# Softmaxed k times v: head pairs on the full array, or single heads on half of its columns

## The chip, the cores and the metric

The kernel runs on one core of one Trainium2 chip. The metric is device microseconds of one execution; before the change three runs gave 1338.9, 1341.31 and 1343.43 us, median 1341.31 us.

## The reference, cut to what matters

Attention with two softmaxes and no score matrix, then two MLPs over all 4608 tokens. Eight batches, eight heads each, 576 positions, 64 columns per head:

```python
q_s = softmax(q, axis=-1)           # over the 64 columns of a head
k_s = softmax(k, axis=2)            # over the 576 positions
kv  = np.einsum('bhsd,bhse->bhde', k_s, v)      # 64 x 64 for each batch and head
x   = np.einsum('bhsd,bhde->bhse', q_s, kv)     # then tokens x 512
h   = x @ w_in;   x = (relu(h) + alpha * min(h, 0)) @ w_out      # 512 -> 2048 -> 512
h   = x @ w_in2;  out = layer_norm(h * softmax(h)) * g @ w_out2  # 512 -> 1024 -> 512
```

## The kernel before

The instructions are written into a tile framework whose scheduler sets the order on each engine; each engine then works strictly in that order. Code order, buffer counts and the scheduler's own idea of what an operation lasts decide it.

The attention of batch 0 runs first, by itself (lines 781 to 833). The attention of batches 1 to 7 is cut into steps (`attention`, line 686) that line 718 (`slot`) strews between the matmuls of the first MLP's first phase: `g1` (lines 330 to 367) makes the hidden layer, `g2` (lines 421 to 432) adds it into the accumulators `acc`. Those matmuls carry single precision as two reduced parts, high and low, in three products.

For each batch and each group of four heads: `k_max` and `k_col` (lines 537 to 553) find the column maxima of k, with two transposes `mt` on TensorE; `k_exp` (line 555) spreads them with two transposes `mb` and writes e = exp(k - max). `k_v` (line 570) is what the change touches. The 576 positions lie as five slices r of 128 partitions, the last half filled with zeros in v. For two head pairs j and five slices r it multiplies the slice of e for two heads (128 columns, the stationary operand) with the slice of v for the same two heads (2 x 65 columns, the moving operand; the 65th column is ones and gives the softmax sum). The result of a pair is 128 x 130 in PSUM, tile `kv`: head one with its own v is the upper left quarter, head two with its own v the lower right one, and the other two quarters mix two heads and are not read. That is 10 matmuls in a `k_v`, and 16 `k_v` in the kernel. VectorE then adds 1e-9 to the sums (line 588), inverts them (589) and writes the two quarters, normalised, into `kvF` (592); `put` (line 123) splits that into the high and low halves `kk`, on ScalarE (124) and VectorE (125). `q_x` (line 657) multiplies `kk` with the transposed q (`qT`, from the transposes `qtp` of line 648) into `xp`, in the three matmuls of lines 662 to 664, the last of which needs the low half.

Batch 0's q softmax, second half, runs on ScalarE as 24 small activations (line 612).

Of the kernel before, what the change touches and what calls it, by code (L numbers as in the profile page):

```python
# [19 lines left out]
def attention_then_two_mlps(  # L20
# [32 lines left out]
    V, S, G, T = nc.vector, nc.scalar, nc.gpsimd, nc.tensor  # L53

    B, H, SQ, D = q.shape
# [21 lines left out]
    KB = SQ // P + 1  # L77
# [45 lines left out]
    def put(hi, lo, src, eng=V):  # L123
        S.activation(hi, src, AF.Copy)  # L124
        eng.tensor_tensor(lo, src, f32(hi), ALU.subtract)  # L125
# [375 lines left out]
    kts, vts = [kt, kt], [vt, vt]  # L501
# [68 lines left out]
    def k_v(b, g):  # L570
        et = A.pop(("e", b, g))
        js = slice(2 * g, 2 * g + 2)
        if g == 0:
            A["kk", b] = at.tile([P, 2, NP, P], F32R, tag="kk", name=f"kk_{b}")
        kk = A["kk", b]
        rk = at.tile([P, 2], F32, tag="rk", bufs=2, name=f"rk_{b}_{g}")
        t = ps_at.tile([P, 2, 2, D1], F32, tag="at", name=f"kv_{b}_{g}")
        for j in range(2):
            for r in range(KB):
                T.matmul(  # L580
                    t[:, j].rearrange("p a e -> p (a e)"),
                    et[:, r, 2 * j:2 * j + 2, :].rearrange("p h d -> p (h d)"),
                    vts[g][:, 2 * j:2 * j + 2, r, :],
                    start=r == 0, stop=r == KB - 1,
                )
        for a in range(2):
            pp_ = slice(a * D, (a + 1) * D)
            V.tensor_scalar_add(rk[pp_, :], t[pp_, :, a, D], 1e-9)
        V.reciprocal(rk, rk)
        for a in range(2):  # L590
            pp_ = slice(a * D, (a + 1) * D)
            V.tensor_tensor(
                kvF[pp_, js, a * D:(a + 1) * D], t[pp_, :, a, 0:D],
                rk[pp_, :].unsqueeze(2).to_broadcast([D, 2, D]), ALU.mult,
            )
        put(kk[:, 0, js], kk[:, 1, js], kvF[:, js])
# [89 lines left out]
    def attention(b):  # L686

        return [
            [lambda: k_max(b, 0)],
            [lambda: k_col(b, 0), lambda: q_max(b, 0)],  # L690
            [lambda: k_exp(b, 0), lambda: load_k(b, 1), lambda: q_exp(b, 0), lambda: load_q(b, 1)],
            [lambda: k_v(b, 0), lambda: load_v(b, 1), lambda: q_sum(b, 0)],
            [lambda: q_norm(b, 0), lambda: k_max(b, 1)],
            [lambda: k_col(b, 1), lambda: q_tr(b, 0, (0, 1)), lambda: q_max(b, 1)],
            [lambda: k_exp(b, 1), lambda: load_k(b + 1, 0), lambda: q_x(b, 0, (0, 1)),
             lambda: q_tr(b, 0, (2, 3)), lambda: q_exp(b, 1), lambda: load_q(b + 1, 0)],
            [lambda: k_v(b, 1), lambda: load_v(b + 1, 0), lambda: q_sum(b, 1)],
            [lambda: q_x(b, 0, (2, 3)), lambda: q_norm(b, 1)],
            [lambda: q_tr(b, 1, (0, 1))],
            [lambda: q_x(b, 1, (0, 1)), lambda: q_tr(b, 1, (2, 3))],  # L700
            [lambda: q_x(b, 1, (2, 3))],
        ]
# [108 lines left out]
    for g in range(2):  # L811
        k_v(0, g)
# [553 lines left out]
```

## Time and profile before

| what | value |
|---|---|
| median of three runs | 1341.31 us |
| the profiled execution, its span (the page gives no other time of its own) | 1341.7 us |
| TensorE busy | 1293.7 us, 96% |
| VectorE, ScalarE busy | 77%, 65% |
| mean granted TensorE clock | 0.987 |

TensorE's busy time counts each matmul from its start to a modelled end, and matmuls overlap: how fast they really follow each other is the distance between starts. A merged row of x20 matmuls lasts from the first start to the last end, so the distance between starts is its length less one matmul's length, over 19. A float32 matmul that is no transpose shows as two rows of the trace, two passes, each with its own weight load; a transpose and the matmuls of the MLPs show as one.

### The profile page before, as it was taken

The numbers are of one execution on the slowest core, as the hardware profiler recorded it, in microseconds if no ns is written. First come the engines' busy times: TensorE is split into PE (matmuls) and PEld (weight loads), VectorE is DVE, ScalarE is ACT, GpSimd is POOL, SyncE is SP. The second block draws the span as 40 slices with busy tenths as digits, with TensorE's granted clock in tenths as the row PEclk, the third lists the DMA queues.
The fourth block names the chain that finished last, engine by engine and source line by source line (L and its number), as shares of the span: only waits on it lengthen the run. The fifth ranks groups of instructions, "written<-read, shape, count | busy, mean of one in ns | idle before, by whom it ended". The sixth has DMA issues, their size and how long they took to land.

```text
span 1341.7 us, 21750 instructions
## 1 busy us (share of the span) xinstructions
PE 1293.7 (96%) x8188; PEld 1150.0 (86%) x8188; DVE 1036.5 (77%) x1796; ACT 865.7 (65%) x1499; POOL 23.0 (2%) x48
## 2 busy tenths in 40 slices
PE   4899999999999999999999999999999999999997
PEld 3788898888888898888888888898889898998887
DVE  6789999778795689667898898765777768686874
ACT  5776565556565668656676766554677776777774
POOL 0000000000000000000000000000000000000000
PEclk9699999999999999999999999999999999999999
DMA  8574645433433342314647575469743433434021
GB/s 189 165 204 119 169 128 139 142 98 108 127 87 121 128 156 95 116 74 177 228 176 251 206 250 198 147 217 341 248 128 100 114 111 112 113 106 118 25 64 32
DMA packets 187160, 195.42 MB, mean 146 GB/s; under 512 B 57392, under 2 KB 156720, under 8 KB 183856
## 3 DMA queue, kind: packets, MB, share of 16 engines
q1 hardware_dynamic: 187056, 194.04, 47.1%
q8 instruction: 64, 1.05, 0.3%
q14 instruction: 40, 0.33, 0.1%
HBM read 122.70 MB, written 71.30 MB: 145 GB/s over the span
## 4 chain that ended last, share of the span: by engine, by line
PE 72%; DVE 10%; DMA 9%; ACT 5%; issue 2%; SPq 1%; POOL 0%; DVEq 0%; ACTq 0%; POOLq 0%
PE acc L430 7%; PE acc L431 7%; PE acc L432 7%; PE ga L334 3%; PE ga L336 3%; PE ga L335 3%; PE gx L334 2%; PE gx L335 2%; PE gx L336 2%; PE oa L1176 2%; PE tp L1129 2%; PE oa L1178 2%; PE h2a L1053 2%; PE h2a L1055 2%; PE h2a L1054 2%
## 5 line engine op out<-in xcount | busy, mean ns | idle before, releaser
L430 PE MATMUL acc<-gg,w 128*128 128x512 f32 x576 | 228.4, 397 | 2.0 <-DVE part L489 1.8
L431 PE MATMUL acc<-gg,w 128*128 128x512 f32 x576 | 229.4, 398 | 0.0
L432 PE MATMUL acc<-gg,w 128*128 128x512 f32 x576 | 228.0, 396 | 0.0
L430 PEld LDWEIGHTS acc<-gg,w 128*128 128x128 f32 x576 | 108.3, 188 | 23.6 <-DVE part L489 3.0
L432 PEld LDWEIGHTS acc<-gg,w 128*128 128x128 f32 x576 | 108.2, 188 | 23.6
L431 PEld LDWEIGHTS acc<-gg,w 128*128 128x128 f32 x576 | 108.2, 188 | 20.7 <-DVE gg L125 0.3
L411 DVE SCALAR_TENSOR_TENSOR t<-rn,nalpha,t 128x512 f32<-128x512 f32 x120 | 85.0, 747 | 36.6 <-ACT t L408 36.5
L124 ACT ACTIVATE gg<-t 128x1024 fp32r<-128x1024 f32 x72 | 76.4, 1061 | 36.0 <-DVE t L411 27.4
L125 DVE TENSOR_TENSOR gg<-t,gg 128x1024 fp32r<-128x1024 f32 x72 | 87.6, 1217 | 8.9 <-ACT gg L124 8.4
L407 ACT ACTIVATE rn<-t 128x1024 f32<-128x1024 f32 x60 | 63.1, 1052 | 44.1 <-DVE t L396 43.5
L125 DVE TENSOR_TENSOR l<-tp,l 128x512 fp32r<-128x512 f32 x55 | 37.7, 685 | 62.1 <-ACT l L124 62.1
L334 PE MATMUL ga<-xT,w_S 128*128 128x256 f32 x240 | 69.4, 289 | 3.8 <-ACT r L340 3.8
L336 PE MATMUL ga<-xT,w_S 128*128 128x256 f32 x240 | 68.2, 284 | 0.0
L335 PE MATMUL ga<-xT,w_S 128*128 128x256 f32 x240 | 68.0, 283 | 0.0
L1098 ACT ACTIVATE el<-el,st 128x1024 f32<-128x1024 f32 x36 | 44.8, 1244 | 29.6 <-DVE st L1097 14.9
L408 ACT ACTIVATE t<-t 128x1024 f32<-128x1024 f32 x60 | 63.0, 1050 | 0.2
L356 PE MATMUL h<-xB,w_c 128*128 128x256 f32 x192 | 55.6, 291 | 0.0
L355 PE MATMUL h<-xB,w_c 128*128 128x256 f32 x192 | 55.3, 292 | 0.0
L357 PE MATMUL h<-xB,w_c 128*128 128x256 f32 x192 | 55.3, 290 | 0.0
L334 PEld LDWEIGHTS ga<-xT,w_S 128*128 128x128 f32 x240 | 45.3, 189 | 7.6 <-ACT r L340 6.1
L1139 ACT ACTIVATE fA<-tp 128x512 f32<-128x512 f32 x51 | 30.9, 605 | 32.1 <-PE tp L1129 32.1
L1089 ACT ACTIVATE el<-hs,st 128x1024 f32<-128x1024 f32 x36 | 41.5, 1154 | 10.6 <-DVE st L1088 10.2
(346 smaller groups left out, 4151.6 us busy)
## 6 DMA issues: line engine op xcount, KB each, us to landing
xraw<-x_d SPq DMA_DIRECT2D x16, 1024.0 KB, 4.8
y_d<-yo_S SPq DMA_DIRECT2D x32, 512.0 KB, 6.0
y_S<-y_d SPq DMA_DIRECT2D x64, 256.0 KB, 3.4
y_d<-yo_A SPq DMA_DIRECT2D x24, 512.0 KB, 3.3
y_A<-y_d SPq DMA_DIRECT2D x48, 256.0 KB, 3.2
q<-in_q_dram SPq DMA_DIRECT2D x16, 576.0 KB, 5.6
p_d<-pt SPq DMA_DIRECT2D x36, 256.0 KB, 3.2
part<-p_d SPq DMA_DIRECT2D x9, 1024.0 KB, 6.5
```

Of the source, the lines that this page charges most:

```text
L124: S.activation(hi, src, AF.Copy)
L125: eng.tensor_tensor(lo, src, f32(hi), ALU.subtract)
L334: T.matmul(bank[:, z, :], wh, x[:, 0, c, :], start=first and z == 0, stop=False, **go_on)
L335: T.matmul(bank[:, z, :], wh, x[:, 1, c, :], start=False, stop=False, **go_on)
L336: T.matmul(bank[:, z, :], wl, x[:, 0, c, :], start=False, stop=c == 1, **go_on)
L356: T.matmul(out, w[:, 0, c, :], x[:, 1, c % 2, :], start=False, stop=False, **go_on)
L407: S.activation(rn, t, AF.Relu, scale=-1.0)
L408: S.activation(t, t, AF.Relu)
L411: V.scalar_tensor_tensor(t[:, j, :], rn[:, j, :], nalpha[:, fg + j:fg + j + 1], t[:, j, :], ALU.mult, ALU.add)
L430: T.matmul(a, wh, g[:, 0, :], start=u == 0 and f == 0, stop=False)
L431: T.matmul(a, wh, g[:, 1, :], start=False, stop=False)
L432: T.matmul(a, wl, g[:, 0, :], start=False, stop=u == NU - 1 and f == FU - 1)
```

## The change

The matmul over a head pair becomes two, one for each head: 64 columns of e stationary, 65 columns of v moving, result 64 x 65. The result of the first head goes to partitions 0 to 63, that of the second to partitions 64 to 127, at the places that were read before; the two mixed quarters are no longer written. In the built program the 160 matmuls on the whole array (128 rows x 128 columns) are 320 on a part of it of 128 rows x 64 columns, in turn at column 0 and at column 64. All others stay on the whole array.

```diff
         t = ps_at.tile([P, 2, 2, D1], F32, tag="at", name=f"kv_{b}_{g}")
         for j in range(2):
             for r in range(KB):
-                T.matmul(
-                    t[:, j].rearrange("p a e -> p (a e)"),
-                    et[:, r, 2 * j:2 * j + 2, :].rearrange("p h d -> p (h d)"),
-                    vts[g][:, 2 * j:2 * j + 2, r, :],
-                    start=r == 0, stop=r == KB - 1,
-                )
+                for a in range(2):
+                    T.matmul(
+                        t[a * D:(a + 1) * D, j, a, :], et[:, r, 2 * j + a, :], vts[g][:, 2 * j + a, r, :],
+                        start=r == 0, stop=r == KB - 1,
+                    )
```

From line 585 on, the changed kernel's lines are one lower. The scheduler also orders the attention of batches 1 to 7 anew; TensorE's order is the same again from row 1988 of 7511 on. On TensorE, in the second `k_v` of batch 1 (`kv`; `qtp` and `minus` are the split of the transposed q), before:

```order
L648 MATMUL qtp_0_3_834<-ident,qe_0_651 128x96 x3
L639 MATMUL qtp_0_2_829<-qT_0_2_828,minus 128x288
L430 MATMUL acc_0_3_999<-gg_0_0_0_754,w_0_1_237 128x512
L431 MATMUL acc_0_3_999<-gg_0_0_0_754,w_0_1_237 128x512
L432 MATMUL acc_0_3_999<-gg_0_0_0_754,w_0_1_237 128x512
L580 MATMUL kv_1_851<-vt,e_1_811 128x130 x2
L639 MATMUL qtp_0_3_834<-qT_0_3_833,minus 128x288
L580 MATMUL kv_1_851<-vt,e_1_811 128x130 x8
L355 MATMUL h_0_0_1_1122<-xB_0_0_382,w_1_c_565 128x256
```

And with the change:

```order
L355 MATMUL h_0_0_1_1162<-xB_0_0_406,w_1_c_585 128x256
L356 MATMUL h_0_0_1_1162<-xB_0_0_406,w_1_c_585 128x256
L581 MATMUL kv_1_881<-vt,e_1_841 64x65 x4
L638 MATMUL qtp_0_3_864<-qT_0_3_863,minus 128x288
L581 MATMUL kv_1_881<-vt,e_1_841 64x65 x16
L357 MATMUL h_0_0_1_1162<-xB_0_0_406,w_1_c_585 128x256
L355 MATMUL h_0_0_1_1162<-xB_0_0_453,w_1_c_585 128x256
```

The matmuls of `k_v` stay one block (this one alone is parted, by one matmul, in both), and the block stands 11 rows later, behind matmuls of the next hidden tile. On VectorE, from the sums of the first `k_v` of batch 1 to its low half `kk` (`mx` is the maximum over the next k, `t` the hidden layer), before:

```order
L588 TENSOR_SCALAR rk_0_678<-kv_0_679 64x2 x2
L542 TENSOR_TENSOR mx_1_706<-mx_1_706,kt 128x256
L589 RECIPROCAL rk_0_678<-rk_0_678 128x2
L125 TENSOR_TENSOR w_1_c_565<-w32b,w_1_c_565 128x512
L592 TENSOR_TENSOR kvF<-kv_0_679,rk_0_678 64x2x64 x2
L542 TENSOR_TENSOR mx_1_706<-mx_1_706,kt 128x256
L119 TENSOR_SCALAR r_2_1_884<-r_2_1_884 128x512
L125 TENSOR_TENSOR kk_677<-kvF,kk_677 128x256
```

And with the change:

```order
L587 TENSOR_SCALAR rk_0_698<-kv_0_699 64x2 x2
L540 TENSOR_TENSOR mx_1_736<-kt 128x256
L588 RECIPROCAL rk_0_698<-rk_0_698 128x2
L367 SCALAR_TENSOR_TENSOR t_0_0_1_999<-rn_0_0_1_1001,nalpha,t_0_0_1_999 128x512
L591 TENSOR_TENSOR kvF<-kv_0_699,rk_0_698 64x2x64 x2
L542 TENSOR_TENSOR mx_1_736<-mx_1_736,kt 128x256
L125 TENSOR_TENSOR w_1_c_585<-w32b,w_1_c_585 128x512
L125 TENSOR_TENSOR kk_697<-kvF,kk_697 128x256
```

The same number of operations stands between, but other ones, in another order: the hidden layer's `t` of line 367 has moved in and the weight load's line 119 out.

## Rows read from the trace of the kernel before

**Rows 1.** The page's engines, TensorE and VectorE by slice, and granted clock.
```profile
PE 1293.7 (96%) x8188; PEld 1150.0 (86%) x8188; DVE 1036.5 (77%) x1796; ACT 865.7 (65%) x1499; POOL 23.0 (2%) x48
...
PE   4899999999999999999999999999999999999997
...
DVE  6789999778795689667898898765777768686874
...
PEclk9699999999999999999999999999999999999999
```

**Rows 2.** Windows by stage: window, busy us (instructions) by engine, clock, DMA.
```profile
core 0: us, PE busy (x) PEld busy (x) DVE busy (x) ACT busy (x) POOL busy (x), PEclk, DMA share, GB/s
...
30.00:54.00 24.00, 20.08 (x75) 16.48 (x76) 17.34 (x21) 17.44 (x52) 0.00 (x0) 0.50 0.62 166
...
60.00:230.00 170.00, 167.47 (x1158) 150.38 (x1158) 160.28 (x270) 108.04 (x198) 0.00 (x0) 1.00 0.58 153
230.00:405.00 175.00, 168.34 (x1107) 150.22 (x1106) 144.22 (x226) 102.32 (x164) 0.00 (x0) 0.99 0.40 109
```

**Rows 3.** TensorE's waits, 56 to 450 us: us in total, times, longest.
```profile
PE mt L550 <- DVE mx L543: 3.5, 4, 1.9
PE xp L664 <- DVE kk L125: 3.3, 3, 1.5
PE kv L580 <- ACT e L567: 0.9, 1, 0.9
```

**Rows 4.** All instructions on tile kv: count, ns least/median/most, first and last start.
```profile
L580 PEld LDWEIGHTS kv<-vt,e x320: 186/188/338, 17.6 to 399.6; 128*128 128x128 f32 x160
L580 PE MATMUL kv<-vt,e x320: 272/273/557, 17.7 to 399.7; 128*128 128x130 f32 x160
```

**Rows 5.** Timeline of TensorE around the last k_v: start us, length us.
```profile
397.46 0.28 PE L335 MATMUL gx<-xB,w_c 128*128 128x256 f32 x1
397.58 2.40 PE L580 MATMUL kv<-vt,e 128*128 128x130 f32 x20
399.73 0.37 PE L336 MATMUL gx<-xB,w_c 128*128 128x256 f32 x1
399.94 0.28 PE L334 MATMUL ga<-xT,w_S 128*128 128x256 f32 x1
400.05 0.28 PE L335 MATMUL ga<-xT,w_S 128*128 128x256 f32 x1
```

**Rows 6.** Transposes of q: one instruction (56 to 450 us), then six in the timeline.
```profile
L648 PE MATMUL qtp<-ident,qe x168: 243/246/367, 76.1 to 420.3; 96*128 96x96 f32 x168
...
238.42 0.66 PE L648 MATMUL qtp<-ident,qe 96*128 96x96 f32 x6
238.86 0.36 PE L334 MATMUL ga<-xT,w_S 128*128 128x256 f32 x1
239.06 0.28 PE L335 MATMUL ga<-xT,w_S 128*128 128x256 f32 x1
```

**Rows 7.** Timeline of the start, batch 0's two k_v and what follows.
```profile
17.65 4.67 PE L580 MATMUL kv<-vt,e 128*128 128x130 f32 x20 [0.24 <-issue]
...
21.86 1.25 ACT L567 ACTIVATE e<-e 128x1280 f32<-128x1280 f32 x1
...
23.21 4.13 PE L580 MATMUL kv<-vt,e 128*128 128x130 f32 x20 [0.88 <-issue]
...
27.32 0.33 ACT L612 ACTIVATE qe<-q,qm 96x64 f32<-96x64 f32 x1
...
27.65 0.40 ACT L124 ACTIVATE kk<-kvF 128x256 fp32r<-128x256 f32 x1
28.56 0.42 ACT L124 ACTIVATE kk<-kvF 128x256 fp32r<-128x256 f32 x1 [0.51 <-DVE kvF L592]
```

## The prediction

> **What bounds the kernel now.** I read the page first, then windows by stage, TensorE's waits, the matmuls of tile kv, and the timeline around one block of them. The page shows TensorE busy in 96% of the span at nearly full clock [rows 1]; busy time counts overlapping matmuls, so by itself it proves little. The windows place the change: from 60 to 405 us, where 14 of the 16 k_v lie, TensorE is busy in 167.47 of 170 and 168.34 of 175 us [rows 2], and the waits that end late there come to a few us in all: 3.5 for the maxima of k, 3.3 for the low half kk, 0.9 for e [rows 3]. So TensorE sets the pace, and a microsecond taken out of its stream is worth nearly one at the end. But VectorE is a close second: from 60 to 230 us it works 160.28 of 170 us [rows 2], its nines in the page's slices [rows 1]. At the start of the kernel it is different: single waits rule [rows 7].
>
> **What a k_v costs now.** The tile's list has 320 matmuls and 320 weight loads: 160 float32 matmuls of two passes, 20 passes to a k_v [rows 4]. The last block lasts 2.40 us with a last pass of 0.273, so starts are (2.40 - 0.273)/19 = 0.112 us apart [rows 4, 5]. 130 columns at 2 cycles of 2.4 GHz are 0.108: the passes follow at the rate at which columns stream, the loads hidden behind them. The matmul after the block starts 0.02 us after the last pass and the one behind it at 399.94, 0.12 (an MLP matmul's usual distance, 399.94 to 400.05) after that pass has streamed at 399.82 [rows 5]: leaving the block costs nothing. A block is 20 x 0.112 = 2.24 us, 14 of them 31.4 us.
>
> **What it costs after.** 40 passes of 65 columns. One pass streams 0.112/2 = 0.056 us. If the two column halves work side by side, a pair takes 0.056 and the block 20 x 0.056 = 1.12 us; a distance of 0.028 between starts is possible, since the row after the block started 0.02 after the pass before it [rows 5]. If they take turns, the block is 40 x 0.056 = 2.24, as before. The weight loads double from 20 to 40, with 64 columns each. The trace has no load of 64 columns. It has loads of 128 columns every 0.083 us: six transposes of q in 0.66, one of them 0.246, so (0.66 - 0.246)/5 [rows 6]; and for float32 that isn't transposed one every 0.112 [rows 5]. So a load of 64 takes between nothing that shows and, if its time doesn't fall with the columns, 0.083 to 0.112; the half of these is 0.042 to 0.056. I take it as hidden, the state in which every load of rows 5 is, and keep the rest for the range.
>
> New, too, is the change of the array's division before and after each block; no row shows one. The nearest, the change from transposes to MLP matmuls, costs 0.02: the six transposes have streamed at 238.42 + 6 x 0.083 = 238.92, 0.12 for the MLP matmul behind them makes 239.04, and the next start is 239.06 [rows 6]. The other end is that the array runs empty: a pass's 0.273 less its 0.112, 0.16 us, twice a block. I take 0.32 a block, since the division differs from its neighbours on both sides; that is dear. A block is then 1.12 + 0.32 = 1.44 us, the gain 0.80, times 14 11.2 us.
>
> The Trainium skill's page "TensorEngine Tiling (Array Packing)", section Tiling Modes, says both things: tiles load and multiply in parallel, and a change of mode (not merely of tile) drains the engine. No row here can show the first; the second is why I price both ends, and without it the gain would be 15.7.
>
> **The start.** The clock is low there: 4.67 us for 20 passes is 0.23 a pass [rows 7], against 0.112 later. The first block's gain is hidden: the second waits for e, whose exponential runs on ScalarE from 21.86 to 23.11 [rows 7]. The second would end about 2 us earlier, but ScalarE stands in its 24 small activations until 27.65, then makes the first kk until 28.05; the second kk starts at 28.56 after a wait of 0.51 [rows 7]. So the start gains at most 0.5, which I take.
>
> **The rest of the edit.** VectorE's and ScalarE's operations are the same in number and shape, and nothing more is moved by DMA. The two unwritten quarters were read by nobody. The scheduler's new order moves blocks by some rows: in batch 1 the second goes behind eleven more rows. Price between both signs: the waits for kk, mx and e are 7.7 us in all now [rows 3]; if all went it would be -7.7, if they doubled +7.7. I take 0, as the same operations stand between the sums and kk, and keep 3 either way.
>
> **Sum.** 11.2 + 0.5 = 11.7 us off the profiled execution's 1341.7 gives 1330.0. The span lies 0.4 above the median of the runs, less than they scatter: forecast 1330, own range 1324 (no price for the division, 15.7 + 0.5, rounded by the order) to 1340 (loads that show in part: 0.046 between starts, the block 2.16).
>
> **Rivals.**
> 1. The halves take turns. In one stream a pass waits for its own half's pass before it, as high and low passes of one head stand next to each other, and the trace has never two matmuls streaming at once. For it: distances are those of the columns everywhere [rows 5, 6]. Against it: the two heads write different partitions and share no weights. Price: 40 x 0.056 = 2.24, plus 0 to 0.32 a block: 1341 to 1346, say 1344. This is also the case that the change doesn't do what it says.
> 2. Slower, by weight loads. Each pass has its own load and there are twice as many. If a load of 64 columns takes the array or its path as long as one of 128, a pass comes every 0.083 at the least [rows 6]: 40 x 0.083 = 3.32 us, + 1.08 and 0.32 for the division = + 1.40 a block, 14 blocks 19.6, and the start, at the low clock and unhidden, some 3 more: 1364. At 0.112 [rows 5] it would be 40 x 0.112 = 4.48 and some 35 us. It decides from the point where passes lie over (2.24 - 0.32)/40 = 0.048 apart. For it: 0.112 may be the load as well as the stream; the row can't part them. Against it: 0.083 for 128 columns makes 0.042 for 64, if columns count.
> The Trainium skill's page "TensorE: Matmul & The Clock Gate", Part 3 (packing small matmuls), has a rule for this: a weight load overlaps running matmuls only when the row group differs. Here all tiles use all 128 rows, so every load would lie bare, 0.056 + 0.042 = 0.098 a pass by [rows 5, 6], 3.92 us a block and some 28 us in all with the division, 1370. The trace disagrees for the whole array, where 20 loads hide in each block; whether it holds for halves no row shows.
> 3. VectorE takes over, or the new order eats the gain. The 8 blocks before 230 us give TensorE 6.4 us, but VectorE has only 9.7 us free there [rows 2], and its order mixes kk with the hidden layer. If those 6.4 are lost: 1336; with 3 us of longer waits for kk: 1339.
>
> **How the numbers follow.** The forecast has 0.44, rival 1 0.24, rival 2 0.19, rival 3 0.13. A difference under 0.3%, 4 us, can't be told from none here. Faster: 0.42 of the forecast and 0.04 of rival 3, 0.46. Same: 0.02, 0.16 and 0.07, 0.25. Slower: 0.08 of rival 1, all of rival 2, 0.02 of rival 3, 0.29. The range reaches from 1324 to 1356: it holds the forecast, rivals 1 and 3 and the milder end of rival 2, and leaves out most of rival 2.
>
> **What would show it.** In the changed kernel's list for tile kv: 640 passes; the row of x40 in the timeline. 1.1 to 1.2 us for it means side by side; 2.2 to 2.3 taking turns; 3.3 and more rival 2. The matmul after the block shows the price of the division, by how late it starts. TensorE's waits for mx, kk and e from 60 to 405 us, and VectorE's busy share to 230 us, show rival 3; the second kk of batch 0 near 28.05 shows the start. If the clock rises later than it did, at 54 us after a stretch at half of it [rows 2], the start's sum fails, by up to half the delay. The forecast is wrong if passes lie further apart than 0.046.

## The result and the profile after

The changed kernel takes 1328.95 us in the median, the kernel before 1341.9 beside it on the same chip: ratio 0.9901, 95% interval 0.9874 to 0.9928 (all ratios below are to the kernel before, measured beside each run), so some 13 us less. One further execution of it, at 1386 us with a granted clock of 0.855, is left out. The forecast was 1330. The time came out; the account of where it comes from did not, and the runs below show that nearly half of the 13 us is the scheduler's new order and not the shorter blocks.

First what each block of k_v became. All instructions on tile kv of the changed kernel (count, ns least/median/most, first and last start), then the timeline around the last block:

```profile
L581 PEld LDWEIGHTS kv<-vt,e x640: 132/138/232, 17.7 to 384.2; 128*64 128x64 f32 x160
L581 PE MATMUL kv<-vt,e x640: 219/222/370, 17.8 to 384.3; 128*64 128x65 f32 x160
```

```profile
382.79 0.39 PE L430 MATMUL acc<-gg,w 128*128 128x512 f32 x1
383.11 1.39 PE L581 MATMUL kv<-vt,e 128*64 128x65 f32 x40
384.43 0.38 PE L334 MATMUL ga<-xT,w_S 128*128 128x256 f32 x1
384.64 0.28 PE L335 MATMUL ga<-xT,w_S 128*128 128x256 f32 x1
```

Twice as many passes as in [rows 4], each 0.222 us long instead of 0.273. In the block the 40 starts spread over 1.39 - 0.222 = 1.17 us, 0.030 apart, where a pass that streams alone would need 0.056: two halves stream at once, a pair every 0.058, and 40 weight loads hide behind them. The ends cost something now. The MLP matmul before the block starts at 382.79 and streams 0.23, so the block could begin at 383.02; it begins at 383.11. After it the second MLP matmul starts at 384.64, the usual 0.12 behind which the array is free puts the block's end at 384.52. From 383.02 to 384.52 it holds TensorE 1.50 us, against 2.24 in [rows 5]: 0.74 less.

The start (timeline, idle time and releaser in brackets) against [rows 7]:

```profile
17.77 2.44 PE L581 MATMUL kv<-vt,e 128*64 128x65 f32 x40 [0.24 <-issue]
...
27.77 0.70 ACT L124 ACTIVATE kk<-kvF 128x256 fp32r<-128x256 f32 x2
...
30.53 0.61 PE L661 MATMUL xp<-qT,kk 128*128 128x288 f32 x1 [0.25 <-ACT qT L639]
```

The blocks take 2.44 us and, at 23.33, 2.08 instead of 4.67 and 4.13, and both kk run in one piece from 27.77 to 28.47, where the second ended at 28.98.

Busy time by stage, as in [rows 2], and TensorE's waits from 56 to 450 us, as in [rows 3]:

```profile
30.00:54.00 24.00, 20.08 (x84) 16.47 (x84) 16.35 (x20) 18.10 (x55) 0.00 (x0) 0.56 0.60 166
60.00:230.00 170.00, 166.97 (x1346) 147.66 (x1345) 162.26 (x272) 107.42 (x200) 0.00 (x0) 1.00 0.59 153
230.00:405.00 175.00, 170.27 (x1283) 150.81 (x1282) 147.82 (x231) 106.67 (x171) 0.00 (x0) 1.00 0.42 116
```

```profile
PE mt L550 <- DVE mx L543: 3.2, 4, 1.1
PE qtp L647 <- DVE qe L633: 2.5, 2, 1.4
PE acc L431 <- DVE gg L125: 1.2, 1, 1.2
PE xp L661 <- ACT kk L124: 0.6, 1, 0.6
```

Here is the first hint that something is missing from the forecast's account. In the two stages after 60 us TensorE should be idle more or less as before if its saving went straight into the time, and it is: 7.8 us of 345 against 9.2. But the waits are not the same ones: those on the low half kk and on e are gone, and qtp and acc wait instead. The order has changed what waits for what.

### The profile page after: what moved, and what is told of

Its sections match the earlier page's. It is cut to its first block, busy times and chain, and to the rows that moved or that the text cites. A ratio compares the mean times of both kernels' runs of the same rounds, so it can differ in the third digit from the quotient of the medians.

```text
span 1328.1 us, 22397 instructions
## 1 busy us (share of the span) xinstructions
PE 1275.7 (96%) x8508; PEld 1129.9 (85%) x8508; DVE 1035.6 (78%) x1796; ACT 862.7 (65%) x1499; POOL 22.9 (2%) x48
## 4 chain that ended last, share of the span: by engine, by line
PE 69%; DVE 12%; DMA 9%; ACT 7%; issue 2%; POOL 0%; SPq 0%; DVEq 0%; ACTq 0%; POOLq 0%
PE acc L431 7%; PE acc L432 7%; PE acc L430 7%; PE ga L334 3%; PE ga L336 3%; PE ga L335 3%; PE gx L334 2%; PE gx L336 2%; PE gx L335 2%; PE oa L1175 2%; PE h2a L1052 2%; PE oa L1177 2%; PE tp L1128 2%; PE h2a L1054 2%; PE h2a L1053 2%
```

## The experiments

### Do the halves run side by side, and what is a us of TensorE worth?

In e1 the two heads' loops are exchanged, so that all passes of one half precede all of the other:

```
 for j in range(2):
-    for r in range(KB):
-        for a in range(2):
+    for a in range(2):
+        for r in range(KB):
             T.matmul(t[a * D:(a + 1) * D, j, a, :], ...)
```

> The changed kernel with the loops over head and slice swapped: five matmuls on one column half, then five on the other, instead of in turn. Everything else, the order on every engine too, is that of the changed kernel. Theory (neighbouring matmuls on different halves run side by side): the side-by-side work goes, passes lie 0.056 us or more apart, a block of 40 takes about 2.24 instead of 1.17 us plus the same 0.27 for the change of division, 14 x 1.07 = 15 us more, with the start 15 to 18: 1344 to 1347. Rival 1 (a pass of 64 x 65 is cheap by itself, neighbours don't matter): the block stays at 1.2 us, 1329. Rival 2 (the gain came from the scheduler's new order or the clock, not from the blocks): the blocks get longer but the time stays within 4 us of 1329.

It took 1333.05 us, ratio 0.9931 (0.9906 to 0.9957): far below the theory's 1344, and at the edge of rival 2's 4 us. The last block in its timeline:

```profile
384.63 2.02 PE L581 MATMUL kv<-vt,e 128*64 128x65 f32 x40
386.57 0.39 PE L334 MATMUL ga<-xT,w_S 128*128 128x256 f32 x1
386.79 0.28 PE L335 MATMUL ga<-xT,w_S 128*128 128x256 f32 x1
```

The halves still pair up in part: (2.02 - 0.222)/39 = 0.046 from start to start, not 0.056, so TensorE starts a pass of the second half before the first half's later ones. Measured as above, the block holds TensorE about 2.13 us (the MLP matmul before it starts at 384.31, so it could begin at 384.54, and it ends 0.12 before 386.79), only 0.11 less than a whole block. Yet the kernel is 0.7% faster than the one before. Its instructions stand in the order of the changed kernel, so shorter blocks can't be the reason for most of it. That made the order itself the suspect.

In e4 every pair is multiplied twice, which doubles the passes; the scheduler made an order of its own for it.

```
+            for twice in range(2):
                 for r in range(KB):
                     for a in range(2):
```

> Every pair of heads is multiplied twice over on halves, the second time writing over the first: 80 passes in a block in place of 40, same result, no more changes of division, the scheduler's order slightly different. Theory (TensorE sets the pace from 60 to 405 us, what a block takes is paid at the end): 14 x 1.17 = 16.4 us more than the changed kernel, with the start 17 to 19: 1346 to 1348. Rival (VectorE is close enough up to 230 us that TensorE has room there): the 8 blocks before 230 us are hidden, 7 to 9 us more: 1336 to 1338.

1353.66 us, ratio 1.0079 (1.0051 to 1.0107), outside both expectations: 14 blocks of about 1.2 us more should cost 16 us over the changed kernel, and it cost 25. I first read it as waits of the longer stream; e12 below points to the order.

### The start

e3 leaves batch 0's two k_v whole and divides the rest (order as in the changed kernel); e3b divides only batch 0's (order as before).

```
+                if b == 0:      # e3;  e3b: if b > 0
+                    T.matmul(t[:, j]..., et[:, r, 2 * j:2 * j + 2, :]..., vts[g][:, 2 * j:2 * j + 2, r, :], ...)
+                    continue
                 for a in range(2):
```

> Batch 0's two k_v go back to head pairs on the whole array, the 14 others stay on halves, in the changed kernel's order. Theory: the start gave about 0.5 us by kk and perhaps 1 to 2 by a clock that rose 2.8 us earlier; 1329.5 to 1331, and the clock rises near 54 us again. Rival: a good part of the 13 us came from the start (clock): 1333 or more.

> Only batch 0's two k_v on halves, the 14 others as before, in the order of before. Theory: 0.5 to 2.5 us faster than before, 1339 to 1341.5, the first x matmul (line 661 here) about 0.5 us earlier than 31.05 us. Rival (the start gave a good part of the gain): 1337 or less.

e3: 1332.81 us, ratio 0.9932 (0.9910 to 0.9954), 4 us above the changed kernel. e3b: 1338.06, ratio 0.9979 (0.9962 to 0.9996), 2.8 us below the kernel before, interval 0.5 to 5.1. Both point to more than the 0.5 us forecast, some 2 to 4, but neither is firm: e3's interval overlaps the changed kernel's, and e3b's reaches down to 0.5.

The traces show less, and not of the division alone. From the start of the first block to the first product with kk it takes 13.40 us before (17.65 to 31.05) and 13.44 in e3, against 12.76 in the changed kernel (17.77 to 30.53) and 12.82 in e3b: 0.6 us. But e6 (next part), whose blocks are all whole, also takes 12.76. Its second block ran in 2.47 us, nearly the 2.40 of the last block in [rows 5], and not in 4.13:

```profile
16.96 4.62 PE L580 MATMUL kv<-vt,e 128*128 128x130 f32 x20 [0.24 <-issue]
22.51 2.47 PE L580 MATMUL kv<-vt,e 128*128 128x130 f32 x20 [0.93 <-issue]
...
29.72 0.61 PE L662 MATMUL xp<-qT,kk 128*128 128x288 f32 x1 [0.25 <-ACT qT L640]
```

So what the division saves here depends on TensorE's speed in that execution when the second block runs. The clock's later rise doesn't tell whole blocks from divided ones either. From 30 to 54 us the granted clock is 0.56 in the changed kernel where it was 0.50 in [rows 2], since it rises at 51.1 us and not at 53.9; in e6, with whole blocks, it is 0.54.

### Order and matmul apart

Instructions of one engine can be held in a given order by an edge from each to the next, which asks for no wait. With a list of the order in which the scheduler put TensorE's, VectorE's, ScalarE's and SyncE's instructions in one of the two kernels, the other kernel's instructions were held in it, one for one; two halves take the place of a whole matmul (code shortened). What the edges cost by themselves has no run of its own. The nearest is e11 below, which is held in the changed kernel's order but for six places: 0.9916 against 0.9901, with intervals that overlap.

```
+    for eng, seq in table.items():
+        for cur in (instructions of eng, by seq):
+            tc.add_manual_dep(cur, prev.name, DependencyInfo(NoSync, DATA), reason="order")
+            prev = cur
```

> The half-column matmuls of the change, with the instructions of TensorE, VectorE, ScalarE and SyncE held in the order that they have in the kernel before, one for one (each whole matmul's place is taken by its two halves). Theory A, the new order carries a part of the 13 us: the earlier runs paid only a quarter to a half of a us for each us that TensorE was kept longer, so 14 shorter blocks give 14 x 0.74 x (1/4 to 1/2) = 2.6 to 5.2 us and the start about 2 us: 1334 to 1338 us. Rival B, all of it is the shorter blocks: 1341.8 - 10.4 - 2 = 1329 us (1327 to 1331). Rival C, the new order costs time: under 1326 us. In the trace each block of 40 passes takes 1.17 us from first start to last start by all three.

> The whole-array matmuls of the kernel before, with the instructions of the four engines held in the order of the changed kernel. Theory A (the order carries a part): 1334 to 1338 us. Rival B (all from the shorter blocks): 1340 to 1344 us. Rival C (the new order costs time): over 1344 us. Blocks of 20 passes at 0.112 us by all three.

| | order of before | order of after |
|---|---|---|
| whole matmuls | 1 (kernel before) | e6: 1334.83 us, 0.9952 (0.9937 to 0.9966) |
| halves | e5: 1342.67 us, 1.0011 (1.0000 to 1.0022) | 1328.95 us, 0.9901 (0.9874 to 0.9928) |

In the old order the halves gain nothing at all. In the new order they gain 0.0051 of 1341, 6.8 us (about 4 either way), and the new order alone, without any divided matmul, gains 6.4 (4.6 to 8.4). e6 came out in theory A's range; e5 lies above the ranges of all three theories.

e5 contains e3b's divided start. If e3b's 2.8 us are real, the 14 other blocks on halves must cost some 4 us in the old order (1.0011 less 0.9979, about 2.7 us either way). Why they should cost time, rather than bring nothing, stays open.

What became of the saved time is in two views. Busy time by stage of e5, then its waits, then the waits of e6:

```profile
60.00:230.00 170.00, 163.91 (x1317) 143.80 (x1316) 160.31 (x269) 107.10 (x197) 0.00 (x0) 0.99 0.59 153
230.00:405.00 175.00, 165.52 (x1221) 145.24 (x1220) 143.55 (x224) 101.06 (x162) 0.00 (x0) 0.98 0.40 108
```

```profile
PE mt L550 <- DVE mx L543: 8.7, 5, 2.4
PE xp L663 <- DVE kk L125: 2.4, 3, 1.3
```

```profile
PE xp L662 <- ACT kk L124: 1.2, 1, 1.2
...
PE mt L550 <- DVE mx L543: 0.7, 3, 0.2
```

In e5 TensorE is idle 15.6 us of the 345, where it was idle 9.2 in [rows 2], and its waits for the maxima of k (mt behind mx) have gone from 3.5 in [rows 3] to 8.7. VectorE did the same amount in the same time: 303.9 us against 304.5. TensorE got done earlier and waited for the next k. In the new order with whole matmuls (e6) that wait is 0.7 us, and TensorE is idle 3.7 us of the 345. That is 5.5 us less than before, most of the 6.4 that the order gains, and it leaves a stream of work to shorten.

The chain of waits says it most plainly. It is followed back from the kernel's last instruction, at each step to what released it or to the instruction before it on its engine. These are its lines between 56 and 405 us, by share of these 349 us, of the kernel before, of e5, of e6 and of the changed kernel (a line ends where the view cuts it):

```profile
by line: PE acc L430 7.4%; PE acc L431 7.4%; PE acc L432 7.4%; DMA q<-in_q_dram 5.3%; PE kv L580 5.1%; DMA kt<-in_k_dram 5.1%; PE h L356 3.9%; DVE qm L601 3.9%; PE qtp L648 3.8%; PE h L357 3.8%; PE h L355 3.8%; issue 2.3%; PE ga L336 2.1%;
```

```profile
by line: DMA kt<-in_k_dram 8.0%; PE acc L432 6.9%; PE acc L431 6.9%; PE acc L430 6.9%; DVE qm L600 3.8%; PE qtp L647 3.5%; DMA q<-in_q_dram 3.3%; PE h L357 3.0%; PE h L356 2.9%; PE h L355 2.9%; DVE qs L626 2.9%; issue 2.5%; PE kv L581 2.4%;
```

```profile
by line: PE acc L431 10.0%; PE acc L432 10.0%; PE acc L430 9.6%; PE kv L580 6.6%; DMA kt<-in_k_dram 4.1%; PE qtp L648 4.0%; PE h L356 4.0%; PE h L357 3.8%; PE h L355 3.8%; PE ga L334 2.8%; PE ga L336 2.8%; PE ga L335 2.7%; PE gx L336 2.2%;
```

```profile
by line: PE acc L432 8.9%; PE acc L431 8.9%; PE acc L430 8.6%; DMA kt<-in_k_dram 5.2%; PE qtp L647 4.1%; PE h L355 3.7%; PE h L356 3.7%; DMA q<-in_q_dram 3.6%; PE h L357 3.6%; PE kv L581 2.7%; PE ga L334 2.5%; PE ga L336 2.5%; DVE qm L600 2
```

Look at kv and at kt, the load of k. Before, kv has 5.1%, 17.8 us: of the blocks' 31.4 us a little over half lies on the chain, the rest beside it. With halves in the old order kv falls to 2.4% and the load of k rises from 5.1 to 8.0%, 10 us more: the chain has gone over to another path. With whole matmuls in the new order kv has 6.6%, 23.0 us, and shortening it by a third (0.74 of 2.24) is worth up to 7.6 us; the measured 6.8, which includes the start and is uncertain by 4, agrees with it. That other path, a piece of e5's chain with start and length:

```profile
109.89 0.12 PE mt L550
...
110.04 0.42 DVE mc L552
...
112.12 1.40 DVE e L563
...
113.54 3.97 DMA kt<-in_k_dram
...
117.93 0.42 DVE mx L540
```

The maxima go through TensorE (mt), VectorE reduces them (mc) and subtracts them from k (e, L563), with other work of its queue between; when that has read k's buffer, the next k is fetched, 4 us, and its maxima begin. The product of k and v is no member of this loop: it comes after e. So where the loop sets the pace, a shorter k_v buys nothing. That the loop is what holds e5 is read from the chain and the waits; no run made the load or the maxima themselves faster.

### Which engine's order is it?

The list of the changed kernel for TensorE alone, that of before for the other three, with halves (e9) and whole (e10):

> Halves; TensorE's instructions in the order of the changed kernel, those of VectorE, ScalarE and SyncE in the order of the kernel before. In the last runs halves in the old order of all four engines gave 1342.7 us, with TensorE waiting 8.7 us for the row maximum of k (mt behind mx) between 56 and 420 us, against 3.2 us in the changed kernel. In the new order the attention's matmuls stand up to 27 places later in TensorE's row, behind more of the MLP's. Theory A, the place of the attention's matmuls in TensorE's row carries it: 1328 to 1332 us, mt's waits 2 to 4 us. Rival B, the earlier place of the other engines' work (the row maximum on VectorE, the loads of k on SyncE) carries it: 1339 to 1343 us, mt's waits 6 us or more. Between the two: both.

> Whole-array matmuls; TensorE's order of the changed kernel, the other three engines' of the kernel before. Whole matmuls gave 1341 us in the old order of all four and 1334.8 in the new. Theory A: 1333 to 1336 us. Rival B: 1339 to 1343 us.

1363.49 us (1.0173, 1.0155 to 1.0192) and 1363.79 us (1.0177, 1.0160 to 1.0194): outside both theories. TensorE's longest waits from 56 to 450 us in e9:

```profile
PE xp L663 <- DVE kk L125: 7.1, 4, 2.8
PE mt L550 <- DVE mx L543: 6.4, 7, 1.9
```

TensorE's row doesn't carry the gain by itself; against the others' old rows it loses 23 us. From 60 to 405 us TensorE is idle 30.4 us in e9, against 9.2 before, in waits for kk (7.1 us, and 5.4 in e10; 3.3 in [rows 3]), for the maxima and for many others. The four rows are one plan. And again halves and whole take the same time, to 0.3 us. The chains of e10 (whole) and e9 (halves) between 56 and 405 us:

```profile
by line: PE acc L431 7.6%; PE acc L432 7.4%; PE acc L430 7.0%; PE kv L580 5.6%; DMA q<-in_q_dram 5.1%; PE h L355 3.8%; PE h L356 3.7%; PE h L357 3.6%; issue 3.5%; DVE qm L601 3.4%; PE qtp L648 2.9%; DMA kt<-in_k_dram 2.6%; DVE qe L615 2.5%;
```

```profile
by line: PE acc L431 6.7%; PE acc L432 6.4%; PE acc L430 6.3%; DMA kt<-in_k_dram 6.2%; DMA q<-in_q_dram 5.3%; DVE qm L600 4.3%; issue 3.8%; PE qtp L647 2.8%; PE h L355 2.7%; PE h L356 2.6%; PE h L357 2.6%; DVE qe L614 2.5%; DVE mx L542 2.3%
```

As between the kernel before and e5, the load of k takes kv's place (2.6 to 6.2%). So the share on the chain is only the most that can be gained: with 5.6% here and 5.1% before the halves bring nothing, with 6.6% in e6 some 7 us. The reverse mixture, TensorE's old row with the others' new ones, was not run.

e12 holds the halves in the order that the scheduler had made for e4:

> Halves once each, in the order that the scheduler made for the earlier run with every pair multiplied twice, that is for blocks twice as long as these. It differs from both orders known so far. Theory A, halves gain only in an order that was made for blocks of their length, and where the order was made for longer ones the saved TensorE time goes into waits, as in the old order (1342.7 us): 1338 to 1345 us. Rival B, the old order is a bad one of its own and others let the halves gain: 1327 to 1334 us.

1354.87 us, ratio 1.0116 (1.0097 to 1.0135), above both expectations, and no less than e4 with twice the passes (1353.66). Its chain between 56 and 405 us and its longest wait:

```profile
by line: DMA kt<-in_k_dram 8.4%; issue 4.3%; PE acc L430 4.3%; PE acc L431 4.3%; PE acc L432 4.2%; DVE qe L614 4.2%; DVE qs L626 3.9%; DMA q<-in_q_dram 3.4%; DVE qm L600 3.4%; PE qtp L647 3.3%; DVE e L563 3.2%; DVE t L411 2.3%; DVE t L367 2
```

```profile
PE mt L550 <- DVE mx L543: 15.8, 7, 3.6
```

kv isn't among the lines that the view shows of its chain. TensorE waits 15.8 us for the maxima. So e4's 25 us were the order's and not the doubled work's, and the rule of the two-by-two table holds a third and a fourth time: the order sets how much of k_v counts. That is nothing in e4 against e12, e9 against e10 and before against e5. In e6 against the changed kernel it is 6.8 us, of which the start may have 2 to 4, so a quarter to a half of the 14 blocks' 10.4.

### Can the remaining waits be filled?

e11 is the changed kernel with its order, but with ready MLP matmuls put ahead of the waiting transposes at six places.

> The changed kernel with its order, but at six places where TensorE's waits are longest in its trace (74.6, 123.3, 285.5, 314.9, 340.6 and 369.6 us) the two to twelve MLP matmuls that stand right behind the waiting transposes (mt or qtp) go ahead of them: 0.47 + 0.47 + 1.45 + 0.60 + 1.30 + 0.60 = 4.9 us of ready work against waits of 0.59, 0.86, 1.58, 1.24, 1.16 and 1.20 us. If TensorE's time counts in full there: 1324 to 1325.5 us. If, as the earlier runs had it, a quarter to a half of it: 1326.5 to 1328 us. If VectorE or the loads of k set the pace, so that later transposes are paid for: 1328.5 to 1331 us.

1329.99 us, ratio 0.9916 (0.9900 to 0.9932): no gain is seen. The place at 285 us, in the changed kernel and in e11:

```profile
285.48 0.69 PE L647 MATMUL qtp<-ident,qe 96*128 96x96 f32 x6 [1.44 <-DVE qe L633]
285.95 0.37 PE L334 MATMUL ga<-xT,w_S 128*128 128x256 f32 x1
...
288.08 0.38 PE L550 MATMUL mt<-ident,mx 128*128 128x128 f32 x2
```

```profile
284.58 0.66 PE L647 MATMUL qtp<-ident,qe 96*128 96x96 f32 x6
...
285.58 0.28 PE L335 MATMUL gx<-xB,w_c 128*128 128x256 f32 x1
287.10 0.41 PE L550 MATMUL mt<-ident,mx 128*128 128x128 f32 x2 [1.24 <-DVE mx L543]
```

The twelve matmuls ga stand ahead and the wait of 1.44 us before qtp is gone; 2.5 us on, mt waits 1.24 us for the maxima of k, where it had waited for nothing. The wait has moved to the next thing that comes from VectorE, and from 60 to 405 us TensorE is idle 7.5 us in all, where it was 7.8. The full 4.9 us of the first theory is excluded; a gain of 1 or 2 us is less than the comparison can show (about 4 us either way). None of the runs is measurably faster than the changed kernel.

### The price of dividing the array

Both runs use the changed kernel's order. In e7 a group's first head pair goes by halves and then the second by whole matmuls; in e8 the two alternate row by row. (e8's alternation changes the sums in kv; it stands here for its time alone.)

```
-        for j in range(2):
-            for r in range(KB):
-                (halves of pair j)
+        for r in range(KB):          # e8;  e7: j outside, r inside
+            (halves of pair 0)
+            (whole matmul of pair 1)
```

> Order of the changed kernel; of each group's two head pairs the first goes by halves (20 passes in 10 pairs), then the second by whole-array matmuls (10 passes): one change of the array's division into halves and one back a group, as in the changed kernel. First start to last start: 10 x 0.058 + 0.10 to 0.19 for the change + 9 x 0.112 = 1.69 to 1.78 us. The time lies between the changed kernel's and that of whole matmuls in the same order.

> The same instructions in the same order of the engines, but for each of the five rows of a group: two halves of the first pair, then the whole matmul of the second: five changes to halves and five back a group in place of one. If a change to halves and back costs some 0.27 us, as the block's two ends in the changed kernel show together, the block is longer than that of the run with one change by 4 x 0.27 = 1.1 us. If the ends' cost comes from something that stands only at a block's ends (the copy after it, the wait for the last result), it is longer by under 0.3 us.

The last block in the timeline, of e7 and of e8:

```profile
386.72 0.80 PE L582 MATMUL kv<-vt,e 128*64 128x65 f32 x20
387.46 1.38 PE L587 MATMUL kv<-vt,e 128*128 128x130 f32 x10
388.59 0.36 PE L334 MATMUL ga<-xT,w_S 128*128 128x256 f32 x1
```

```profile
404.70 0.34 PE L580 MATMUL kv<-vt,e 128*64 128x65 f32 x4
...
407.71 0.49 PE L584 MATMUL kv<-vt,e 128*128 128x130 f32 x2
407.96 0.37 PE L334 MATMUL ga<-xT,w_S 128*128 128x256 f32 x1
```

The same 30 passes, from the first to the matmul after them: 1.87 us with one change to halves and back, 3.26 with five. (3.26 - 1.87)/4 = 0.35 us for going there and back. The changed kernel's block agrees: 1.50 less 20 pairs of 0.058 is 0.34. The kernels took 1334.12 and 1354.93 us, in one execution each: of the 20.8 us between them 14 x 1.39 = 19.5 are these blocks. Between these two executions the longer blocks are paid nearly in full, whereas e6 against the changed kernel gave only a part of theirs back.

## Why the prediction was right, and where it was wrong

- **The halves work side by side: right.** A pair every 0.058 us against 0.056 forecast, every load hidden. The Trainium skill's page "TensorE: Matmul & The Clock Gate", Part 3, says that a weight load overlaps running matmuls only when the row group differs, which would have had the 64-column loads lie bare here, since all tiles use the same rows. At 0.030 us from start to start with one load each, this trace disagrees with it.
- **The price of the division: the right size.** 0.32 us a block was estimated from a pass's 0.273 less its 0.112, at both ends; 0.34 to 0.35 was measured, twice. That the array runs empty is the reading behind it; the runs show only the sum. The Trainium skill's page "TensorEngine Tiling (Array Packing)", section Tiling Modes, says that a change of mode drains the engine, and e8 is what such changes cost here.
- **Gain of a block: 0.80 forecast, 0.74 measured.** 14 of them free 10.4 us of TensorE, not 11.2. A small miss of size.
- **"TensorE sets the pace, and a microsecond taken out of its stream is worth nearly one at the end": wrong, the step that failed.** It was read from the busy share and the short waits of [rows 2, 3]. 97% busy doesn't rule out a second path that is nearly as long, and by the chains there is one: the loop from k's load through VectorE. The chain of the kernel before gave a warning that wasn't used: kv has 5.1% there, 17.8 of 31.4 us. In the old order the 10.4 us are worth nothing (e5), and the chain there runs through the loop; in the new order, with the start, they are worth 6.8.
- **The new order, "I take 0, as the same operations stand between the sums and kk": wrong.** It is worth 6.4 us (e6), the largest single term that can be separated. The forecast priced the order by the waits that it could remove, 7.7 us, which was the right size, and then put it at nothing.
- **The start: right for its one dependency, open beyond it.** The first product with kk (L661) starts at 30.53 us, before at 31.05. But the same time was won in e6 with whole blocks, and by e3 and e3b the start may be worth 2 to 4 us, of which the traces account for only a part.
- **The rivals.** Taking turns and bare loads fell with the first block of the trace. "VectorE takes over" happened, but in the old order, which the forecast didn't think of: held in that order, the change is worth nothing (e5).

The sum, 11.7 us, thus came out by luck, from two errors that cancel: too much for the blocks, nothing for the order. (It was also taken off a span and read as a time; times here stand some 2.3 us above their spans, 1330.36 and 1328.1 for the profiled execution after. That is within the scatter.) What stays open is which of the moved instructions carry the order's 6.4 us, and how much of the rest is the start's.

## What to carry to other kernels

Before a shortened piece of work is counted in full, see how much of it lies on the chain of waits in its stage, which is the most that it can bring, and what the next path is: with two paths of nearly the same length, taking 10 us from one can bring nothing. Where a scheduler orders the instructions, a change of a matmul's length is two changes; hold the order fixed and change one at a time before the gain is credited to either. An idle gap that is filled tells nothing yet either: look for the wait that comes next from the same engine.

## What the hardware showed

**The clock fell behind some of TensorE's long waits.** e5's two longest waits (timeline), and the stretches in which the clock fell (windows; the granted clock is the column after POOL):

```profile
265.90 0.41 PE L550 MATMUL mt<-ident,mx 128*128 128x128 f32 x2 [2.26 <-DVE mx L543]
...
379.38 0.66 PE L550 MATMUL mt<-ident,mx 128*128 128x128 f32 x2 [2.36 <-DVE mx L543]
```

```profile
266.40:269.80 3.40, 3.40 (x19) 3.40 (x18) 2.43 (x5) 1.97 (x4) 0.00 (x0) 0.50 0.01 2
379.00:382.40 3.40, 3.02 (x16) 3.05 (x17) 2.92 (x6) 0.41 (x1) 0.00 (x0) 0.51 0.00 0
```

Each time the clock is granted at half, the lower of its two levels, for 3.4 us, so at most 1.7 us more for each; a third such stretch, from 75.3 us, stands behind a wait of 1.85 us. e6, e11 and the changed kernel, whose longest waits there are 1.2 to 1.4 us, keep the full clock from 60 to 405 us; the kernel before has one such stretch, behind a wait of 1.9 us [rows 3]. It doesn't fall behind every such wait: in e4 one of 2.00 us, to 329.74, and in e12 one of 2.12, to 72.21, passed at the full clock (1.00 from 327 to 333 and from 69 to 77 us). So part of what e5's execution loses can be the clock, at most 3.4 us for two stretches more.

**Passes in runs are still paired in part.** In e1, with ten passes of one half ahead of ten of the other, the mean distance was 0.046 us and not 0.056. In the trace's single records of the last block the starts come in pairs, 0.002 to 0.006 us apart, three times about each of the three changes of half, and singly, 0.053 to 0.061 apart, elsewhere (0.107 after the block's first). That is as if the next half's first three passes ran beside the last three of the half before, ahead of the written order; "strictly in that order" above doesn't hold for TensorE's passes here.
